# A fused attention and gated-MLP kernel: first loads spread over three queues, wk released by the landing of x, V's shifted copy by DMA, wd in four gated pieces

## Chip, cores, metric

One core of one Trainium2 chip. The metric is the device time of one execution in microseconds; lower is better.

## The reference, cut

```python
x = A_x                                     # (1, 2048, 512), bf16
g = sigmoid((x * gate_w).sum(-1, keepdims=True))
# A: 32 heads of 16; 4 segments of 512 rows
q, k, v = x @ wq, x @ wk, x @ wv
for s in range(4):
    p = softmax(q_s @ k_s.T * scale + causal_mask);  a_dot = p @ v_s
    a_mem = (phi(q_s) @ M) / (phi(q_s) @ z + 1e-6)      # memory of earlier segments
    o_s = gh * a_mem + (1 - gh) * a_dot
    M += phi(k_s).T @ v_s;  z += phi(k_s).sum(rows)
a = concat(o) @ wo
# B: gated MLP
b = (relu(x @ W_gate) * (x @ W_up)) @ W_down            # 512 -> 1792 -> 512
return g * a + (1 - g) * b
```

## The kernel before

The kernel describes its work as operations with estimated durations; a list scheduler, run when the program is built, gives each engine a fixed order, and the instructions are emitted in it. So a changed estimate, dependency or operation can reorder everything that comes after. TensorE runs in four modes: full 128-row matmuls, scores in four row strips, value products in 64x32 tiles, and column mode, for small products or for full ones cut into four column strips.

```python
MM = 0.216; SW = 0.1                       # a full matmul, a mode change, in us
...
for _ in range(28):                        # warm-up, on a tile that VectorE fills
    nc.tensor.matmul(g_dummy.t[:, 0:P], lhsT=zero[:, 0:P], rhs=zero[:, 0:P], ...)
...
for n, (c0, c1) in enumerate(((0, 1), (1, 2), (2, 4))):     # wq: three loads, GpSimd
    nc.gpsimd.dma_start(out=wq_sb[:, c0:c1, :], in_=A_wq[c0 * P:c1 * P, :]...)
...
o_wk0 = op("wk0", {"DVE": 0.08}, lambda e: nc.vector.memset(wk_sb[0:1, 0, 0:1], 0.0), ...)
lw["wk"].deps.append((o_wk0, None))        # wk is loaded after this write ...
o_wk0.deps.append((xc0[0][0], None))       # ... which follows the first copy of x transposed
...
def xload(s, key):                         # SyncE: x of a segment, transposed, then plain
    nc.sync.dma_start_transpose(out=xT[s].t[:], in_=x[s * L:(s + 1) * L, :])
    nc.sync.dma_start(out=xn[s].t[:], in_=...)
...
nc.sync.dma_start(out=wd_sb[:], in_=wview(B_W_down))        # wd: one load
...
nc.vector.scalar_tensor_tensor(xn[s].t[:, t, :], xn[s].t[:, t, :], 1.0, gwrep[:], ...)  # gate
...
nc.gpsimd.tensor_copy(VS[s].t[64 * r:64 * r + 64, t, ...], src[:, :, r, 0:DH])  # x 32
```

The softmax here doesn't subtract the row's maximum and nothing guards it: scores larger than these inputs give would overflow.

## Time and profile before

| what | before |
|---|---|
| median of 4 runs | 266.89 us (266.32 to 267.23) |
| span of the profiled run | 265.27 us |
| start, to the first matmul on wk | 9.60 us |
| list, from there to the last matmul's start | 252.26 us |
| end, from there to the end | 3.41 us |

The last three rows add up to the span: TensorE is full, so the start, the price of its list of instructions, and the end make the time.

### The profile page before, as it was taken

Reading aid. Unit: us, or ns where it says so; the run is one execution under the profiler, and the core shown is the slowest. Engines: PE = TensorE matmul, PEld = TensorE weight load, DVE = VectorE, ACT = ScalarE, POOL = GpSimd, SP = SyncE. Lnnn points to the kernel's source line nnn. Section 1 sums busy time; section 2 is a strip of 40 time slices with the busy share of each in tenths; the row PEclk is TensorE's granted clock in tenths of the full one; section 3 lists DMA queues with packets and bytes.
Section 4 is the critical chain, followed back from the end, with each engine's and each line's share of the span. In section 5 each row is a group of like instructions: output and inputs, shape, how many; then the busy total and the mean of one; then the engine's idle time right before and its main releaser. Section 6 shows DMA issues by size and latency. Waiting matters only on the chain.

```text
span 265.3 us, 7048 instructions
## 1 busy us (share of the span) xinstructions
PE 257.0 (97%) x2808; PEld 115.9 (44%) x2844; DVE 183.8 (69%) x407; ACT 193.9 (73%) x189; POOL 191.0 (72%) x470
## 2 busy tenths in 40 slices
PE   8999999999999999999999999999999999999995
PEld 6433444444454444444434434344443444344444
DVE  1497888888975285998888837688985735566611
ACT  3598999899885558999896668898788566777010
POOL 8678888888559788798648988887878866537000
PEclk9999999999999999999999999999999999999999
DMA  5997990017310100000551010000000010000011
GB/s 162 289 252 203 313 261 13 4 40 80 100 26 1 42 20 22 0 2 2 132 88 23 21 42 20 4 2 0 2 0 4 0 42 23 20 2 0 2 41 40
DMA packets 27057, 15.54 MB, mean 59 GB/s; under 512 B 13584, under 2 KB 26896, under 8 KB 27024
## 3 DMA queue, kind: packets, MB, share of 16 engines
q1 hardware_dynamic: 26304, 14.30, 22.0%
q0 software_dynamic: 176, 0.52, 0.6%
q8 instruction: 22, 0.36, 0.6%
q10 hardware_dynamic: 544, 0.26, 0.3%
q14 instruction: 11, 0.09, 0.1%
HBM read 9.84 MB, written 2.10 MB: 45 GB/s over the span
## 4 chain that ended last, share of the span: by engine, by line
PE 97%; issue 2%; DVE 0%; ACT 0%; DVEq 0%
PE G L248 74%; PE S L738 9%; PE G L849 7%; PE G L246 3%; PE S L406 2%; PE G L291 1%; PE G L611 1%; PE G L785 0%; PE G L385 0%; DVE os L700 0%; ACT xT L395 0%; DVE os L253 0%; DVE mcole L268 0%; DVEq L700 0%; DVE mcol L267 0%
## 5 line engine op out<-in xcount | busy, mean ns | idle before, releaser
L752 ACT ACTIVATE E<-S 128x2048 bf16<-128x2048 f32 x72 | 135.1, 1876 | 34.3 <-PE S L738 31.9
L760 POOL TENSOR_SCALAR_AFFINE_SELECT E<-E 64x256 bf16<-64x256 bf16 x256 | 115.7, 452 | 38.5 <-ACT E L752 24.6
L248 PE MATMUL G<-xT,wu_sb 128*128 128x512 bf16 x211 | 57.3, 380 | 0.4 <-issue 0.2
L248 PE MATMUL G<-xT,wg_sb 128*128 128x512 bf16 x206 | 56.2, 380 | 1.1 <-issue 0.8
L663 DVE TENSOR_TENSOR hT<-G,os 128x512 bf16<-128x512 f32 x56 | 38.2, 684 | 19.7 <-ACT os L659 10.7
L248 PE MATMUL G<-wd_sb,hT 128*128 128x512 bf16 (+1 forms) x212 | 48.9, 365 | 1.1 <-issue 1.0
L884 DVE STREAM_TRANSPOSE T<-G 128x512 f32<-128x512 f32 x44 | 30.3, 702 | 14.0 <-PE G L849 8.2
L659 ACT ACTIVATE os<-G 128x512 bf16<-128x512 f32 x56 | 32.7, 597 | 6.1 <-PE G L248 5.3
L248 PEld LDWEIGHTS <-wu_sb 128*128 128x128 bf16 x218 | 19.9, 98 | 24.8 <-issue 3.0
L248 PEld LDWEIGHTS <-wg_sb 128*128 128x128 bf16 x218 | 19.4, 98 | 24.6 <-issue 4.1
L248 PEld LDWEIGHTS <-hT 128*128 128x128 bf16 x222 | 20.3, 98 | 22.3 <-issue 2.6
L738 PE MATMUL S<-QT,K 32*128 32x192 bf16 (+7 forms) x512 | 28.6, 287 | 0.5
L738 PEld LDWEIGHTS <-K 32*128 32x128 bf16 x512 | 8.2, 92 | 30.4 <-issue 29.9
L700 DVE TENSOR_SCALAR os<-G,ngcol 128x512 bf16<-128x512 f32 (+1 forms) x10 | 7.0, 697 | 19.4 <-PE G L248 19.3
L849 PE MATMUL G<-E,Vp 64*32 64x128 bf16 (+7 forms) x512 | 19.0, 284 | 0.2 <-issue 0.2
L849 PE MATMUL G<-E,VS 64*32 64x128 bf16 (+7 forms) x512 | 18.4, 284 | 0.0
L248 PE MATMUL G<-wo_sb,oT 128*128 128x512 bf16 (+1 forms) x66 | 17.2, 367 | 0.3 <-issue 0.3
L597 POOL COPY VS<-Vp 64x256 bf16<-64x256 bf16 x32 | 13.3, 416 | 4.8 <-DVE Vp L515 3.3
L904 DVE TENSOR_TENSOR O<-T,sm 128x256 bf16<-128x256 f32 x32 | 15.8, 524 | 0.3
L248 PE MATMUL G<-xT,wk_sb 128*128 128x512 bf16 x60 | 15.8, 380 | 0.3 <-issue 0.2
L702 ACT ACTIVATE os<-G,ngcol 128x512 bf16<-128x512 f32 x7 | 4.8, 687 | 15.0 <-PE G L248 15.0
L479 POOL COPY R<-rcol 32x4 f32<-32x4 f32 x64 | 13.5, 210 | 3.0
(98 smaller groups left out, 302.0 us busy)
## 6 DMA issues: line engine op xcount, KB each, us to landing
out_dram<-os SPq DMA_DIRECT2D x15, 128.0 KB, 1.7
wd_sb<-in_B_W_down_dram SPq DMA_DIRECT2D x1, 1792.0 KB, 13.4
xn<-in_A_x_dram SPq DMA_DIRECT2D x3, 512.0 KB, 4.7
wg_sb<-in_B_W_gate_dram SPq DMA_DIRECT2D x2, 512.0 KB, 5.8
wu_sb<-in_B_W_up_dram SPq DMA_DIRECT2D x2, 512.0 KB, 6.9
wg_sb<-in_B_W_gate_dram SPq DMA_DIRECT2D x3, 256.0 KB, 6.9
wu_sb<-in_B_W_up_dram SPq DMA_DIRECT2D x3, 256.0 KB, 7.2
wk_sb<-in_A_wk_dram SPq DMA_DIRECT2D x1, 512.0 KB, 4.0
```

Source lines behind the costliest of these rows:

```text
L246: nc.tensor.matmul(out_ap[q], lhsT=lhsT[:, q], rhs=rhs, start=start, stop=stop, tile_position=(0, 32 * j))
L248: nc.tensor.matmul(out_ap, lhsT=lhsT, rhs=rhs, start=start, stop=stop)
L479: nc.gpsimd.tensor_copy(R[s][32 * j:32 * j + 32, k, :], rcol[32 * k:32 * k + 32, cols])
L597: nc.gpsimd.tensor_copy(VS[s].t[64 * r:64 * r + 64, t, 0:H // 2 * HP].rearrange("p (h v) -> p h v", v=HP)[:, :, 0:DH], src[:, :, r, 0:DH])
L659: nc.scalar.activation(rg.t[:], g.t[:], ACT.Relu)
L663: nc.vector.tensor_tensor(h.t[:], u.t[:], rg.t[:], ALU.mult)
L738: nc.tensor.matmul(sp.t[:, j, off:off + w], lhsT=K2[s, cc].t[rows, kb, :, :].rearrange("p r k -> p (r k)"), rhs=QT[s, cc].t[rows, L - w:L] ...
L752: nc.scalar.activation(eb_.t[:], sp.t[:], ACT.Exp, scale=SCALE)
L760: nc.gpsimd.affine_select(out=v, in_=v, compare_op=ALU.is_ge, fill=0.0, base=0, pattern=[[0, 4], [1, 64]], channel_multiplier=-1)
L849: nc.tensor.matmul(gs[r].t[32 * j:32 * j + 32, L - w:L], lhsT=v, rhs=src.t[rows, j, off:off + w], start=(kb == 0), stop=(kb == 7), tile_po ...
L884: nc.vector.transpose(T.t[:].rearrange("p b e -> p (b e)"), g.t[:])
L904: nc.vector.tensor_tensor(O.t[:, :, r, :], T.t[:, :, 0:DH], sm.t[:, r, :, None].to_broadcast([P, 16, DH]), ALU.mult)
```

## The change

Its intent: let TensorE's warm-up begin sooner, get x, wq and wk into place sooner, take 13 us of copies and 2 us of fills off GpSimd, keep the 1.8 MB of wd from blocking small transposes in the queue, and give the scheduler durations closer to the measured ones.

```diff
-MM = 0.216
-SW = 0.1
+MM = 0.2159
+SW = 0.094
+PX = 1.06                       # estimates of GpSimd times this
...
+    ones = nc.const_aps.tensor(1.0, [P, P], BF16)
-        for _ in range(28):      # on a tile filled by VectorE
+        for _ in range(31):      # on the constant
...
-    (x: two parts on SyncE, two on ScalarE; wq: three parts on GpSimd)
+    x0_part(0, 0, "SP", -300)
+    x0_part(0, 1, "ACT", -300)
+    wq_part(0, 1, "ACT", -299)
+    x0_part(1, 0, "SP", -299)
+    x0_part(1, 1, "POOL", -110)
+    wq_part(1, 2, "SP", -298)
+    wq_part(2, 4, "POOL", -80)
...
-    o_wk0 = ... nc.vector.memset(wk_sb[0:1, 0, 0:1], 0.0)      # after the first copy of xT
+    o_wk0 = ... nc.vector.tensor_copy(wk_sb[0:1, 0, 0:1], xn[0].t[0:1, 0, 0:1])   # after x landed
...
-        nc.sync.dma_start(out=wd_sb[:], in_=wview(B_W_down))
+    for c0, c1 in ((0, 4), (4, 8), (8, 12), (12, 14)):
+        gt = op(f"wd{c0}g", {"DVE": 0.08}, ... memset(wd_sb[0:1, c0, 0:1], 0.0) ...)
+        o = load(f"wd{c0}", ... wd_sb[:, c0:c1] ..., deps=[gt])
+    GATES = [(0, 1, 3), (0, 2, 1), (0, 2, 3), (0, 3, 1)]   # each gate waits for this exp
...
+            if ci == 0:          # two more warm-up matmuls ahead of the first on wq
+                for _ in range(2): nc.tensor.matmul(qS.t[:, 0, 0:P], lhsT=ones, rhs=ones, ...)
...
-        (VS: two buffers; 32 copies on GpSimd)
+            for r in range(2):   # one buffer, once a segment
+                nc.sync.dma_start(out=VS[s].t[a], in_=Vp[s].t[b])
```

More of the change, by code (lines that the diff above doesn't have):

```diff
@@ L26 @@
 VW = H * HP + 16
-VSW = H // 2 * HP + 16
-MM = 0.216
-SW = 0.1
+MM = 0.2159
+SW = 0.094
 MG = 1.0
+PX = 1.06
 class Buf:
@@ L63, in op @@
         o.flex, o.ran = flex, mode
+        engs = {e: d * (PX if e == "POOL" else 1.0) for e, d in engs.items()}
         o.name, o.engs, o.emit, o.key, o.cls, o.mode = name, engs, emit, key, cls, mode
@@ L219 @@
     Vpp = pool("Vp", 2, [P, 4, VW])
-    VSp = pool("VS", 2, [P, 4, VSW])
+    VSp = pool("VS", 1, [P, 4, VW])
     Ep = pool("E", 8, [P, 4, L])
@@ L225 @@
     osp = rgp = pool("os", 4, [P, D])
-    zero = osp.tiles[0]
     smp = pool("sm", 3, [P, 2, 16], F32)
@@ L249 @@
     ACTC = lambda n: 0.19 + 0.000833 * n
-    def c_zero(e):
-        nc.vector.memset(zero[:, 0:P], 1.0)
-    o_zero = op("zero", {"DVE": 0.15}, c_zero, cls=0, key=-100)
+    ones = nc.const_aps.tensor(1.0, [P, P], BF16)
+    o_zero = op("zero", {"DVE": 0.15}, lambda e: None, cls=0, key=-100)
     def c_ident(e):
@@ L262, in c_warm @@
     def c_warm(e):
-        nc.scalar.activation(scratch[:], zero[:, 0:1], ACT.Exp)
+        nc.scalar.activation(scratch[:], ones[:, 0:1], ACT.Exp)
     o_warm = op("warm", {"ACT": 1.5}, c_warm, deps=[o_zero], cls=0, key=-100)
@@ L274, in c_vones @@
     def c_vones(e):
-        for t in Vpp.tiles + VSp.tiles:
+        for t in Vpp.tiles:
             nc.gpsimd.memset(t[:].rearrange("p a b -> p (a b)"), 1.0)
-    o_vones = op("vones", {"POOL": 6.2}, c_vones, key=-60)
+    o_vones = op("vones", {"POOL": 4.2}, c_vones, key=-60)
     def c_bdm(e):
@@ L289, in c_dummy @@
     def c_dummy(e):
-        for _ in range(28):
-            nc.tensor.matmul(g_dummy.t[:, 0:P], lhsT=zero[:, 0:P], rhs=zero[:, 0:P], start=True, stop=True)
+        for _ in range(31):
+            nc.tensor.matmul(g_dummy.t[:, 0:P], lhsT=ones, rhs=ones, start=True, stop=True)
     g_dummy = Buf(G)
@@ L312, with first_load, x0_part, wq_part @@
     lx0, lw, lwq = {}, {}, {}
-    for i in range(2):
-        for eng, q, h in (("SP", nc.sync, 0), ("ACT", nc.scalar, 1)):
-            def f(e, i=i, q=q, h=h):
-                q.dma_start(out=xn[0].t[:, 2 * h:2 * h + 2, 256 * i:256 * i + 256],
-                            in_=x[256 * h:256 * h + 256, 256 * i:256 * i + 256].rearrange("(t p) d -> p t d", p=P))
-            lx0[i, h] = load(f"x0_{i}{h}", f, 131072, -300 + i, eng=eng, alloc=[xn[0]] if (i, h) == (0, 0) else [],
-                             uses=[] if (i, h) == (0, 0) else [xn[0]])
-    for n, (c0, c1) in enumerate(((0, 1), (1, 2), (2, 4))):
-        def f(e, c0=c0, c1=c1):
-            nc.gpsimd.dma_start(out=wq_sb[:, c0:c1, :], in_=A_wq[c0 * P:c1 * P, :].rearrange("(c p) n -> p c n", p=P))
-        o = op(f"wq{c0}", {"POOL": 1.0}, f, key=-110 + 15 * n, cls=0, land=131072 * (c1 - c0) / GBs)
+    QUEUE = {"SP": nc.sync, "ACT": nc.scalar, "POOL": nc.gpsimd}
+    def first_load(name, eng, key, nbytes, out_ap, in_ap, alloc=(), uses=()):
+        o = load(name, lambda e: QUEUE[eng].dma_start(out=out_ap(), in_=in_ap), nbytes, key, eng=eng, alloc=alloc, uses=uses)
+        if eng == "POOL":
+            o.engs["POOL"] = 0.9
+        return o
+    def x0_part(i, h, eng, key):
+        first = not lx0
+        lx0[i, h] = first_load(f"x0_{i}{h}", eng, key, 131072,
+                               lambda: xn[0].t[:, 2 * h:2 * h + 2, 256 * i:256 * i + 256],
+                               x[256 * h:256 * h + 256, 256 * i:256 * i + 256].rearrange("(t p) d -> p t d", p=P),
+                               alloc=[xn[0]] if first else [], uses=[] if first else [xn[0]])
+    def wq_part(c0, c1, eng, key):
+        o = first_load(f"wq{c0}", eng, key, 131072 * (c1 - c0), lambda: wq_sb[:, c0:c1, :],
+                       A_wq[c0 * P:c1 * P, :].rearrange("(c p) n -> p c n", p=P))
         for ci in range(c0, c1):
             lwq[ci] = [o]
+    x0_part(0, 0, "SP", -300)
[5 more added lines that the diff above has]
+    wq_part(2, 4, "POOL", -80)
     o_vones.deps.append((lwq[3][0], -1e9))
@@ L334 @@
     lw["wk"] = loadw("wk", wk_sb, A_wk, 0, D, 1)
-    o_wk0 = op("wk0", {"DVE": 0.08}, lambda e: nc.vector.memset(wk_sb[0:1, 0, 0:1], 0.0), key=-490, cls=0)
+    o_wk0 = op("wk0", {"DVE": 0.08}, lambda e: nc.vector.tensor_copy(wk_sb[0:1, 0, 0:1], xn[0].t[0:1, 0, 0:1]), key=-600, cls=0,
+               deps=[lx0[0, 0]], uses=[xn[0]])
     lw["wk"].deps.append((o_wk0, None))
@@ L369 @@
     lwo = loadw("wo", wo_sb, A_wo, 0, D, 3)
-    def f(e):
-        nc.sync.dma_start(out=wd_sb[:], in_=wview(B_W_down))
-    lwd = load("wd", f, P * NF * D * 2, 3)
+    lwd, wd_gate = {}, []
+    for c0, c1 in ((0, 4), (4, 8), (8, 12), (12, 14)):
+        gt = op(f"wd{c0}g", {"DVE": 0.08}, lambda e, c0=c0: nc.vector.memset(wd_sb[0:1, c0, 0:1], 0.0), key=-600, cls=0)
+        wd_gate.append(gt)
+        o = load(f"wd{c0}", lambda e, c0=c0, c1=c1: nc.sync.dma_start(out=wd_sb[:, c0:c1], in_=wview(B_W_down)[:, c0:c1]),
+                 P * (c1 - c0) * D * 2, 3, deps=[gt])
+        for fb in range(c0, c1):
+            lwd[fb] = o
     last_dma[0] = None
@@ L404, in f @@
         def f(e, ci=ci):
+            if ci == 0:
+                for _ in range(2):
+                    nc.tensor.matmul(qS.t[:, 0, 0:P], lhsT=ones, rhs=ones, start=True, stop=True)
             for c in range(NC):
@@ L407, in f @@
                                  start=(ci == 0), stop=(ci == NC - 1))
-        o_q0 = op(f"q0.{ci}", {"PE": 4 * MM * (1.5 if ci < 2 else 1)}, f,
+        o_q0 = op(f"q0.{ci}", {"PE": 4 * MM * (1.2 if ci < 2 else 1)}, f,
                   deps=xc0[ci] + lwq[ci] + [(o_q0, 0.0) if ci else None],
@@ L412 @@
             first_x(ci + 2, o_q0)
-    o_wk0.deps.append((xc0[0][0], None))
     xc0 = [o for c in range(NC) for o in xc0[c]]
@@ L419 @@
             for o in lx[s]:
-                o.deps.append((lwd, -1e9))
+                o.deps.append((lwd[NF - 1], -1e9))
         xr[s] = [lx[s][0]]
@@ L590, in proj_v, with f @@
                        uses=[g, Vp[s]])
-        if t == 0:
+        if t == 3:
             VS[s] = Buf(VSp)
-        o_vs[s, t] = []
-        for r in range(2):
-            def f(e, r=r):
-                src = Vp[s].t[64 - 64 * r:128 - 64 * r, t, 0:H * HP].rearrange("p (h r v) -> p h r v", r=2, v=HP)
-                nc.gpsimd.tensor_copy(
-                    VS[s].t[64 * r:64 * r + 64, t, 0:H // 2 * HP].rearrange("p (h v) -> p h v", v=HP)[:, :, 0:DH],
-                    src[:, :, r, 0:DH])
-            o_vs[s, t].append(op(f"vs{s}{t}{r}", {"POOL": 0.5}, f, deps=[o_v[s, t]] + (o_vs[s, t - 1] if t else []),
-                                 key=a.key + 4, cls=2, alloc=[VS[s]] if t == 0 and r == 0 else [],
-                                 uses=[Vp[s]] + ([] if t == 0 and r == 0 else [VS[s]])))
+            def f(e):
+                for r in range(2):
+                    a, b = slice(64 * r, 64 * r + 64), slice(64 - 64 * r, 128 - 64 * r)
+                    nc.sync.dma_start(out=VS[s].t[a], in_=Vp[s].t[b])
+            o_vs[s] = op(f"vs{s}", {"SP": 1.2}, f, deps=[o_v[s, t] for t in range(4)], key=a.key + 4, cls=0, land=2.5,
+                         alloc=[VS[s]], uses=[Vp[s]])
     W2 = 2 * (DH + 1)
@@ L641, in mz0 @@
         k = dkey(3)
-        a = op("mz0", {"PE": 0.5}, lambda e: mz_mm(0, g), deps=mz_deps(0), key=k, mode="C", alloc=[g], uses=[pK[0], Vp[0]])
+        a = op("mz0", {"PE": 0.56}, lambda e: mz_mm(0, g), deps=mz_deps(0), key=k, mode="C", alloc=[g], uses=[pK[0], Vp[0]])
         mz_after(0, a, g, k)
@@ L685, in dn @@
                 prev = op(f"d{s}{t}{hf}.{p0}", {"PE": (p1 - p0) * MM / halves}, f,
-                          deps=[lwd, (prev, 0.0) if prev else None] + gate + [o_h[s, fb] for fb in range(p0, p1)],
+                          deps=[lwd[p0], (prev, 0.0) if prev else None] + gate + [o_h[s, fb] for fb in range(p0, p1)],
                           key=dkey((p1 - p0) / halves), mode="D", flex="C", alloc=[g] if p0 == 0 else [],
@@ L741, in f @@
                                          tile_position=(32 * j, 0))
-            a = op(f"f{s}{c}.{n}", {"PE": MM}, f,
+            a = op(f"f{s}{c}.{n}", {"PE": 0.229}, f,
                    deps=[o_q[s, cc] for cc in chunks] + [o for cc in chunks for o in o_k2[s, cc]] +
@@ L753, in unit @@
             b = op(f"e{s}{c}.{n}", {"ACT": 1.88}, f, deps=[a], key=kf, cls=0, alloc=[eb_], uses=[sp])
+            if (s, c, n) in GATES:
+                wd_gate[GATES.index((s, c, n))].deps.append((b, None))
             offs = [p[2] for p in parts]
@@ L793, in dens @@
             gm = Buf(G)
-            rec_of[s, "mz"] = am = op(f"mz{s}", {"PE": 0.5}, lambda e: mz_mm(s, gm), deps=[(a, 0.0)], key=k0 - 20, mode="C",
+            rec_of[s, "mz"] = am = op(f"mz{s}", {"PE": 0.56}, lambda e: mz_mm(s, gm), deps=[(a, 0.0)], key=k0 - 20, mode="C",
                                       alloc=[gm], uses=[pK[s], Vp[s]])
@@ L842, in f @@
                     for j in range(4):
+                        h = 8 * c + 2 * j + r
                         if kb % 2 == r:
-                            h = 8 * c + 2 * j + r
                             v = Vp[s].t[rows, kb // 2, h * HP:h * HP + 32]
                         else:
-                            h = 4 * c + j
                             v = VS[s].t[rows, kb // 2, h * HP:h * HP + 32]
@@ L850, in f @@
                                          start=(kb == 0), stop=(kb == 7), tile_position=(64 * r, 32 * j))
-        a = op(f"pv{s}{c}", {"PE": 1.05}, f,
-               deps=[(m, MG) for m in masks] + [o_v[s, t] for t in range(4)] + [o for t in range(4) for o in o_vs[s, t]] +
+        a = op(f"pv{s}{c}", {"PE": 1.015}, f,
+               deps=[(m, MG) for m in masks] + [o_v[s, t] for t in range(4)] + [o_vs[s]] +
                ([(behind, 0.0)] if behind else []),
```

## The prediction

> **What bounds the kernel now.** I read the page of the profile first, then the list of waits for TensorE alone, then the stretches before, in and after its dense work, and last its instructions in order of time at the start. From the page:
>
> ```profile
> PE 257.0 (97%) x2808; PEld 115.9 (44%) x2844; DVE 183.8 (69%) x407; ACT 193.9 (73%) x189; POOL 191.0 (72%) x470
> ...
> PE   8999999999999999999999999999999999999995
> ...
> POOL 8678888888559788798648988887878866537000
> ...
> PE 97%; issue 2%; DVE 0%; ACT 0%; DVEq 0%
> ```
>
> TensorE is busy for 257.0 of 265.3 us, in every slice, and the chain that ended last runs through it for 97%. GpSimd, from which the change takes most, is busy for 72% and stands nowhere in that chain. A busy TensorE need not be at its peak, so I asked what it waited for (total us, times, longest):
>
> ```profile
> PE G L248 <- issue: 2.4, 15, 0.2
> PE G L291 <- DVE mcole L268: 1.1, 1, 1.1
> PE G L849 <- issue: 0.2, 1, 0.2
> ```
>
> After the first 1.1 us it waits for no transfer and for no other engine by any amount worth a row. The stretches (busy us of each engine in each):
>
> ```profile
> 0.00:1.12 1.12, 0.00 (x1) 0.01 (x1) 0.18 (x3) 0.00 (x0) 0.19 (x4) 1.00 0.00 0
> 1.12:9.60 8.48, 8.38 (x59) 5.97 (x61) 1.45 (x13) 3.02 (x6) 8.21 (x9) 1.00 0.73 234
> 9.60:262.10 252.50, 248.62 (x2750) 109.95 (x2783) 181.72 (x390) 190.93 (x183) 182.59 (x458) 1.00 0.22 53
> 262.10:265.30 3.20, 0.03 (x1) 0.00 (x0) 0.48 (x1) 0.00 (x0) 0.00 (x0) 1.00 0.07 20
> ```
>
> So the time is a start of 9.6 us, 252.5 us of TensorE instructions in a fixed order, and 3.2 us for the last eviction and store. A change shortens it only if it makes the start shorter, or the list of TensorE instructions cheaper. The start in order of time (start, duration, engine and line, count):
>
> ```profile
> 1.12 3.17 PE L291 MATMUL G<-os 128*128 128x128 bf16 x28 [1.12 <-DVE mcole L268]
> 4.08 1.06 PE L385 MATMUL G<-ident,xn 128*128 128x128 bf16 x8
> 5.18 1.54 PE L406 MATMUL S<-xT,wq_sb 128*128 128x512 bf16 x4
> 6.56 0.39 PE L385 MATMUL G<-ident,xn 128*128 128x128 bf16 x4
> 6.79 1.03 PE L406 MATMUL S<-xT,wq_sb 128*128 128x512 bf16 x4
> 7.65 0.39 PE L385 MATMUL G<-ident,xn 128*128 128x128 bf16 x4
> 7.87 1.89 PE L406 MATMUL S<-xT,wq_sb 128*128 128x512 bf16 x7
> 9.60 0.38 PE L248 MATMUL G<-xT,wk_sb 128*128 128x512 bf16 x1
> ```
>
> Here too TensorE is full, with one hole of 0.25 us ahead of 5.18. But it works slowly at first: the 28 warm-up matmuls start 107 ns apart, the transposes at 6.56 start 56 ns apart. The first four matmuls on wq take 5.18 to 6.56, the next four 6.79 to 7.65. The trace has the clock at full speed from 6.27 us. The landings of the loads are not in the way: x at 3.5 to 4.6 us, all well ahead of their transposes. Only wk is close: issued at 5.31, landed 4.03 us later at 9.34, and its first weights are loaded at 9.38.
>
> **What the skill says.** "TensorE: Matmul & The Clock Gate", Part 1, has TensorE at half clock until it has been busy through one window of about 3.4 us, which runs freely and does not begin with the kernel; 107 and 56 ns for 128 columns are its figures too, and the trace agrees. "TensorEngine Tiling (Array Packing)", Key Properties, says that changing the tiling mode drains the engine; the trace agrees: from the last full matmul to the first score matmul it is 312 ns, against 216 within a run, so 96 ns more. "DMA: Bandwidth & Descriptors", Rules for kernel authors, says that spreading loads over issuing engines does not add bandwidth and only saves issue time. This trace agrees in so far as an issue on SyncE takes about 0.5 us and loads queued behind each other land one by one.
>
> **The change, part by part.**
>
> *Warm-up.* The warm-up matmuls no longer read a tile that VectorE fills, but a constant written before the program's start. VectorE's fill ran from 0.89 to 1.06, so TensorE should start at about 0.92, 0.2 us sooner. There are 31 in place of 28: 3 x 107 ns = 0.32 us more. The transposes therefore come 0.12 us later; since that shift is in half-speed time, it is worth 0.06 us if the clock rises at the same moment. Two further matmuls of 128 columns (0.21 us) fall into the hole of 0.25 us. Busy 0.2 us sooner, TensorE may see the clock rise up to 0.2 us sooner, worth half: -0.1. Sum about -0.04 us.
>
> *wq and x over three queues.* x landed 0.3 us or more before its use and wq in time, so the reordering takes nothing from the path: 0.
>
> *wk held by the landing of x.* Its gate falls at about 3.6 us instead of 5.26, so it is issued some 1.6 us sooner and should land at 7.7 to 8.4 instead of 9.34. In the profiled run that uncovers only 0.04 us. But in a run where the clock rises sooner than 6.27, the queries would be done before 9.34, and wk would be the floor. Between no gain and about 0.4 us, by where the window falls: I put -0.15 on average.
>
> *V's shifted copy by DMA.* It takes 32 copies (13.3 us) and 2.3 us of fills off GpSimd. None lies on the path: 0. It adds two transfers per segment on SyncE, 64 x 4736 B each, 592 KB together. wk and wv (512 KB each) landed 1.45 us apart, so 592 KB is 1.7 us of transfer; 4.03 - 1.45 = 2.6 us is fixed; 4.3 us from issue to landing.
>
> *wd in four pieces.* It moves traffic out of the way of the transposes of K's features, which it delayed to 6.7 us from issue; TensorE waited for neither. 0.
>
> *The list of TensorE instructions.* The scheduler lays it out anew, and this I counted from the built programs: 2844 matmuls become 2759. Of these +5 are warm-up and -90 are 30 full matmuls that were issued as four column strips and no longer are (34 become 4). The useful work is the same. What a strip run costs shows in these two lines:
>
> ```profile
> 77.72 2.90 PE L246 MATMUL G<-wd_sb,hT 128*32 128x512 bf16 x48
> 80.56 0.40 PE L738 MATMUL S<-QT,K 32*128 32x320 bf16 x8
> ```
>
> 12 split matmuls take 80.56 - 77.72 = 2.84 us; 12 x 0.216 and a mode change of 0.096 are 2.69; 0.15 over. The other three such runs are over by 0.03, 0.03 and 0.01, so 0.22 for 34, and about -0.19 us for the 30 that go. Against this, the number of stretches in one mode rises from 171 to 174, and what follows what: with the trace's price of each kind of change (96 ns full to scores, 120 back, 93 full to value product, 118 scores to value product, 144 scores to strips, 106 strips to scores) the counts before give 18.48 us and after 18.71: +0.22 us.
>
> Sum: -0.04 - 0.15 - 0.19 + 0.22 = -0.16 us; 266.98 becomes 266.8.
>
> **Rivals.** *A new wait on the value copy.* There is now one buffer, so SyncE must wait for the last value product of a segment before it copies the next segment's, and the last transpose of K's features queues behind. In the new order the memory update that needs this transpose follows that product by 23 full matmuls and two score fills: 23 x 0.216 + 2 x 0.43 = 5.8 us. By the sizes above the transpose lands 4.3 + 0.5 = 4.8 us after. One us of slack: if a copy within SBUF ran at half the rate of a load, TensorE would wait about 0.7 us there, making 267.5. The second such place has 8 us.
>
> *The clock rises a whole window sooner.* If starting 0.2 us sooner tipped the window that ended near 2.9 us, the work from 2.9 to 6.3 would run at full speed, except that it waits for x to land at 3.5: up to 1.3 us, 265.6. TensorE was busy for only half of that window, and would be for 0.6 of it; unlikely.
>
> *A schedule that stops fitting.* The order is fixed from estimated durations, and TensorE takes it strictly. Gates for wd on VectorE wait for an exp on ScalarE and could hold evictions up. In the old kernel the same way of estimating left TensorE without waits, so I expect the new one to as well; if not, 268 to 270.
>
> *GpSimd as the real limit.* If its masks had set the pace, 15 us less on it would show as several us. Against it: TensorE has not one wait on it.
>
> **Range and chances.** Three runs of before spread over 0.9 us, which the window of the clock explains in size (3.4 us of phase at half speed is up to 1.7). I take 266.8 with 265.8 to 267.7. Two per cent is 5.3 us; the start as a whole is 9.6 and mostly untouched work, and nothing else is idle: faster 0.01. Slower by 5.3 us needs a broken schedule: 0.02.
>
> **What would show it.** The first warm-up matmul at about 0.9 us; the transposes near 4.2; the moment of the clock's rise, which I cannot place to better than a us; wk landed before 8.5; the first wk matmul at 9.3 to 9.7; strips of full matmuls down to 16; GpSimd busy for about 176 us and the time unmoved; no row for TensorE waiting on a transfer. A wait ahead of a memory update or a value product would show the first rival right; a TensorE total smaller by over 2 us without an earlier clock would prove my prices of the mode changes wrong.

## The result, and the profile after

The changed kernel's median is 267.98 us (267.61 to 268.29, 4 runs) against 266.89: ratio 1.0042, 95% interval 1.0021 to 1.0064, slower by 0.4%. Ratios are the mean time of one kernel's fast runs over that of the other's fast runs of the same rounds, so not quite the ratio of the medians quoted. The direction of the forecast was wrong, and the time lies above the forecast's range, though within 2% as forecast.

What TensorE waited for, in the changed kernel (total us, times, longest):

```profile
PE G L290 <- PEq L1030: 0.8, 1, 0.8
PE S L429 <- DMA wq_sb<-in_A_wq_dram: 0.3, 1, 0.3
PE G L248 <- DVE T L905: 0.2, 1, 0.2
```

The warm-up now starts at 0.83 us, as meant. But there are two new waits: one on wq in the start, and one on VectorE's transposes of value products, which lies in the middle. (The 2.4 us of "issue" in the old list are no waits: in that profile 36 of TensorE's 2844 matmul records are missing, in this one none. So TensorE's busy time and counts of matmuls can't be compared between the two.) The stretches, cut near the same events as before, to a tenth of a microsecond at the end:

```profile
0.83:9.54 8.71, 8.31 (x65) 6.08 (x66) 1.65 (x15) 2.91 (x6) 7.34 (x11) 1.00 0.80 248
9.54:262.50 252.96, 252.70 (x2695) 108.58 (x2693) 180.19 (x392) 192.60 (x185) 167.55 (x420) 1.00 0.26 62
262.50:265.90 3.40, 0.00 (x0) 0.00 (x0) 0.49 (x1) 0.00 (x0) 0.00 (x0) 1.00 0.07 19
```

The dense stretch grew from 252.50 to 252.96 us and the end from 3.20 to 3.40, while the start ends at 9.54 in place of 9.60. (Cut exactly at the last matmul's start, as in the first table, the list grew from 252.26 to 252.68 and the end from 3.41 to 3.69.) GpSimd went from 191.0 to 175.1 us busy, and nothing came of it. The start in order of time:

```profile
0.83 3.46 PE L290 MATMUL G<-const-bfloat16-1.0 128*128 128x128 bf16 x31 [0.83 <-PEq L1030]
...
5.12 1.02 PE L429 MATMUL S<-xT,wq_sb 128*128 128x512 bf16 x4
5.98 0.39 PE L405 MATMUL G<-ident,xn 128*128 128x128 bf16 x4
6.28 1.04 PE L429 MATMUL S<-xT,wq_sb 128*128 128x512 bf16 x4
7.16 0.39 PE L405 MATMUL G<-ident,xn 128*128 128x128 bf16 x4
7.81 1.90 PE L429 MATMUL S<-xT,wq_sb 128*128 128x512 bf16 x8 [0.26 <-DMA wq_sb<-in_A_wq_dram]
9.54 1.24 PE L248 MATMUL G<-xT,wk_sb 128*128 128x512 bf16 x5
```

In this run the clock was up at 4.44 us, 1.8 us sooner than in the profile before, and the first four matmuls on wq took 0.86 us instead of 1.38. That 0.5 us was lost again: the transposes at 7.16 end their starts at 7.32, and the matmuls on the last two blocks of wq begin at 7.81, when wq has landed.

The wait in the middle, in order of time, on VectorE and TensorE:

```profile
135.76 0.90 DVE L483 SCALAR_TENSOR_TENSOR xn<-xn,gwrep 128x512 bf16<-128x512 bf16 x1 [1.18 <-DMA xn<-in_A_x_dram]
...
136.59 0.71 DVE L905 STREAM_TRANSPOSE T<-G 128x512 f32<-128x512 f32 x1
...
136.99 0.38 PE L248 MATMUL G<-pq,M 128*128 128x512 bf16 x1
...
137.35 1.02 PE L248 MATMUL G<-xT,wg_sb 128*128 128x512 bf16 x4
...
138.62 0.38 PE L248 MATMUL G<-xT,wu_sb 128*128 128x512 bf16 x1 [0.25 <-DVE T L905]
```

VectorE stood still for 1.18 us because the plain load of x for the last segment had not landed (issued 129.69, landed 135.74). It could not be issued sooner, since SyncE takes its instructions in order: the transposing load of the same rows, which stands ahead of it, was issued only at 127.75. Behind it in VectorE's order stands the transpose of a value product that had just been finished. That transpose frees an accumulator, and TensorE needs accumulators: against its usual steps it lost 0.15 us after 136.99 and 0.41 after 138.00, together 0.56.

The tail, the last store of each kernel (issue, duration), with the span:

```profile
core 0 of [0], span 265.3 us
262.75 0.33 SPq L708 DMA_DIRECT2D out_dram<-os  x1
```
```profile
core 0 of [0], span 265.9 us
263.11 0.33 SPq L727 DMA_DIRECT2D out_dram<-os  x1
```

From issue to end it is 2.52 us before (first fence) and 2.79 after. The store lands 1.53 and 1.56 us after its issue; the rest is what follows it.

### The profile page after: what moved, and what is told of

Read it like the earlier page. It is cut to its first block, busy times and chain, and to the rows that moved or that the text cites. A ratio compares the mean times of both kernels' runs of the same rounds, so it can differ in the third digit from the quotient of the medians.

```text
span 265.9 us, 6922 instructions
## 1 busy us (share of the span) xinstructions
PE 261.0 (98%) x2759; PEld 114.7 (43%) x2759; DVE 182.3 (69%) x408; ACT 195.5 (74%) x191; POOL 175.1 (66%) x435
## 4 chain that ended last, share of the span: by engine, by line
PE 92%; DMA 4%; DVE 1%; POOL 1%; issue 0%; SPq 0%; POOLq 0%; DVEq 0%
PE G L248 75%; PE S L758 9%; PE G L870 6%; DMA xn<-in_A_x_dram 2%; DMA wq_sb<-in_A_wq_dram 2%; PE S L429 1%; PE G L630 1%; DVE xn L483 1%; DVE T L905 0%; PE G L807 0%; PE G L246 0%; POOL xn L315 0%; DVE os L719 0%; POOL ident L257 0%; POOL ident L256 0%
## 5 line engine op out<-in xcount | busy, mean ns | idle before, releaser
L248 PE MATMUL G<-xT,wu_sb 128*128 128x512 bf16 x224 | 59.8, 380 | 0.2 <-DVE T L905 0.2
L248 PE MATMUL G<-xT,wg_sb 128*128 128x512 bf16 x224 | 59.3, 380 | 0.0
L248 PE MATMUL G<-wd_sb,hT 128*128 128x512 bf16 (+1 forms) x234 | 53.9, 367 | 0.0
L248 PEld LDWEIGHTS <-hT 128*128 128x128 bf16 x234 | 21.4, 98 | 23.7 <-issue 2.8
L248 PEld LDWEIGHTS <-wg_sb 128*128 128x128 bf16 x224 | 20.2, 98 | 25.5 <-issue 3.9
L248 PE MATMUL G<-wo_sb,oT 128*128 128x512 bf16 (+1 forms) x68 | 18.0, 368 | 0.0
L248 PE MATMUL G<-xT,wk_sb 128*128 128x512 bf16 x64 | 16.5, 379 | 0.0
L947 POOL TENSOR_TENSOR O<-O,O 128x512 bf16<-128x512 bf16 x11 | 13.1, 1186 | 4.8 <-DVE O L925 4.1
```

Source lines behind the costliest of these rows:

```text
L248: nc.tensor.matmul(out_ap, lhsT=lhsT, rhs=rhs, start=start, stop=stop)
L947: (nc.vector if e == "DVE" else nc.gpsimd).tensor_tensor(Oa.t[:], Oa.t[:], Ob.t[:], ALU.add)
```

## The experiments

The accounts to test, beside noise. **S**, start: wq lands late, because of where it is issued (S1) or because the early wk takes its bandwidth (S2). **D**: the halt at 137 us comes from VectorE held by x. **L**: the new TensorE order is itself dearer. **T**: the end is longer by its construction. Where I say "TensorE's order is the changed kernel's", I compared the two built programs and they agree instruction by instruction.

### after_again: the changed kernel unaltered

> The changed kernel unaltered, for its spread and a second profile. Its first profile has four terms against the kernel before: first wk matmul 9.54 us against 9.60, the list of TensorE instructions from there to the last matmul 252.7 against 252.3, of which 0.56 is a halt at 137 us, and 3.69 against 3.41 from the last matmul to the end. If the list (theory L) and the halt (theory D: VectorE held by a late x) are systematic, the list is 252.6 to 252.8 again and the halt 0.4 to 0.7 at the same place; if the end (theory T) is systematic, it is over 3.6 again. Theory S, the start: the first wk matmul cannot come before about 9.5 however early the clock rises, because wq comes late. Ratio 1.002 to 1.006.

267.91 us (266.58 to 268.62) against 267.09; ratio 1.0023, interval 0.9999 to 1.0047. The second profile, of a run of 268.62, has start 10.21, list 253.04, end 3.67. The halt is there again, 0.97 us in its two parts, the end too. New is a wait in the start:

```profile
PE G L248 <- DMA wk_sb<-in_A_wk_dram: 1.0, 1, 1.0
```

wk, issued at 3.64, landed only at 10.16. So D and T are systematic, and the new start varies.

### wq_pool: the place of the wq issues undone

```diff
-    wq_part(0, 1, "ACT", -299)
+    wq_part(0, 1, "POOL", -110)
-    x0_part(1, 1, "POOL", -110)
-    wq_part(1, 2, "SP", -298)
+    x0_part(1, 1, "ACT", -299)
+    wq_part(1, 2, "POOL", -95)
```

> The three parts of wq all issued by GpSimd and the fourth part of x by ScalarE, as before the change; TensorE's order is the changed kernel's to the instruction. If the place of the wq issues makes wq late (S1), its last two blocks are in use from at most 7.4 us when the clock rises early, and the first wk matmul comes at 9.2 or sooner, 0.1 to 0.4 us of time gained at most. If it is the early wk that takes their bandwidth (S2), wq's last blocks come at 7.6 or later still and the first wk matmul stays at 9.5 or later. The list stays at 252.7.

267.22 us (266.81 to 268.01), ratio to before 1.0008 (0.9991 to 1.0025). First wk matmul at 9.17 with the clock up at 5.37; wq's last blocks in use from 7.45, without a wait; list 252.68, end 3.70. These look like S1's numbers, but the landings do not bear S1 out: wq's last two blocks landed at 7.38 here, and at 7.76 and 7.11 in the changed kernel's two profiles. TensorE came to them only at 7.45 here, so it did not wait. In time it is 0.7 below the changed kernel of the same rounds, but the two intervals overlap, and the profiles bear out 0.3 of it.

### wk_late: wk's gate undone

```diff
-    ... tensor_copy(wk_sb[0:1, 0, 0:1], xn[0].t[0:1, 0, 0:1]), key=-600 ... deps=[lx0[0, 0]]
+    ... memset(wk_sb[0:1, 0, 0:1], 0.0), key=-490, cls=0)
+    o_wk0.deps.append((xc0[0][0], None))
```

> wk held until the first copy of transposed x, as before the change; the rest is the changed kernel, TensorE's order the same. Under S2 (wk takes wq's bandwidth) the last two blocks of wq land by 7.0 and TensorE has no wait on wq there, but wk itself then lands at 9.2 to 9.4 and is the floor: first wk matmul 9.4 to 9.6, time within 0.2 us of the changed kernel. Under S1 the wait on wq's last blocks stays at 0.2 us or more.

267.69 us (267.32 to 268.54), ratio 1.0028 (1.0009 to 1.0047). wk landed at 9.43 and the first wk matmul came at 9.48 after a wait of 0.2; the wait on wq was gone, and the last packet of GpSimd's loads ended at 6.03 us, against 7.34 and 6.77 in the changed kernel's two profiles. The landings of wq's last two blocks (us) in all 14 profiles tell the two accounts apart:

| | wq over three queues | wq on GpSimd |
|---|---|---|
| wk early | 7.76, 7.11, 7.49, 7.28, 7.26, 6.73 | 7.38, 7.41, 7.33, 6.74 |
| wk late | 6.42 | 6.43, 6.38, 6.30 |

(First row: after, after_again, xn_first, lanes, vs_pool, wd_early; then wq_pool, combined, combined_again, before_start. Second row: wk_late; then before, before_again, before_warm.)

So S2 holds: an early wk delays wq by about 0.9 us, and a late one becomes the floor. S1, the place of the issues, is not shown: it moves the landing by less than the profiles scatter. Taking one gate back changes one wait for another.

### xn_first: the plain load of x ahead of the transposing one

```diff
-            nc.sync.dma_start_transpose(out=xT[s].t[:], ...)
+            (nc.sync.dma_start(out=xn[s].t[:], ...) if s > 1 else None); nc.sync.dma_start_transpose(out=xT[s].t[:], ...)
```

> For the last two segments the plain load of x is issued ahead of the transposing load instead of after it; nothing else moves, and the four engines' orders are those of the changed kernel. Theory D: VectorE no longer waits on x (1.2 us in the changed kernel), the halt of TensorE at 137 to 138.6 us goes, the list takes 252.1 to 252.2 and the time falls by 0.5 to 0.6 us, ratio to before about 1.002. Rival: the halt comes from the value transposes themselves, and 252.7 stays.

266.72 us (266.60 to 267.51), ratio 0.9994 (0.9976 to 1.0012); list 252.13 in place of 252.68, and TensorE's only listed wait is the 0.8 before its first instruction. x is issued at 121.21 and landed at 125.24, nine us ahead of its use. The same TensorE instructions as above:

```profile
136.73 0.38 PE L248 MATMUL G<-pq,M 128*128 128x512 bf16 x1
136.94 1.03 PE L248 MATMUL G<-xT,wg_sb 128*128 128x512 bf16 x4
137.81 0.38 PE L248 MATMUL G<-xT,wu_sb 128*128 128x512 bf16 x1
```

The steps between these three are 0.21 and 0.87 us, against 0.36 and 1.27: 0.55 us regained. D is shown. The time fell by more than that (1.2 in medians of the same rounds); the remainder is within the spread.

### lanes: five more transfers, so that the last store gets another semaphore

```diff
-    lwo = loadw("wo", wo_sb, A_wo, 0, D, 3)
+    lwo = load("wo", ... two halves ...)
-    ... dma_start(out=wd_sb[:, c0:c1], ...)
+    ... each piece as two halves ...
```

> Each of the four wd transfers and the one of wo is issued as two halves; nothing else moves. With five more transfers the last store falls on the last of the eight semaphores that SyncE goes through at the end, in place of the third. Theory T: the end is longer because SyncE, after the last landing, still goes through five waits of 62 ns that are long satisfied; then last matmul to end falls from 3.68 to 3.35-3.42 us, the list stays 252.7 with its halt at 137 us, and the time falls by 0.3. Rival: the store itself lands later in the new kernel; then 3.6 or more stays.

267.06 us (266.12 to 267.91), ratio 0.9995 (0.9968 to 1.0022). The end is 3.33 us, against 3.69 and 3.67; the halt is there, 0.97 us as in after_again (list 253.10), and in this profile the clock rose only at 6.59 (start 9.77). The last store:

```profile
core 0 of [0], span 266.2 us
...
263.76 0.33 SPq L727 DMA_DIRECT2D out_dram<-os  x1
```

2.44 us from issue to end. SyncE's own records tell why. In the built program, the transfers of SyncE and ScalarE use eight semaphores in turn. At the end SyncE waits for them one after the other, a wait every 62 ns even where it is long satisfied. In the kernel before, five such waits ran while the last store was under way and one came after; in the changed one, with more transfers, the last store's semaphore is the first waited for, and five come after. T is shown, and it has nothing to do with the store. Two runs made for other ends agree: wd_early, with three transfers fewer, has the last store on the last semaphore again and an end of 3.32; vs_pool, with eight fewer and so the same semaphore as the changed kernel, has 3.69.

### vs_pool: V's copy back on GpSimd

```diff
-                    nc.sync.dma_start(out=VS[s].t[a], in_=Vp[s].t[b])
+                    nc.gpsimd.tensor_copy(...)          # eight a segment, in one block
```

> The changed kernel with V's shifted copy back on GpSimd (eight copies a segment at the place where SyncE issued its transfer, and a fill of the buffer at the start); TensorE's, VectorE's and ScalarE's orders are the changed kernel's. If GpSimd is off the path, as predicted, the list stays within 0.1 of 252.7 plus or minus what the traffic on SyncE did: theory D2 says that the transfers of V's copy do not cause the halt at 137 us, so it stays at 0.5. Rival: GpSimd's 3.5 us in one block delay masks and hence value products; then TensorE shows waits ahead of them and the list is over 253. GpSimd busy rises by 13 to 16 us.

268.04 us (267.62 to 268.52), ratio 1.0038 (1.0013 to 1.0063); GpSimd busy 190.0 us. My D2 failed: the halt at 137 is gone, since x landed 0.5 us sooner after the first wk matmul and VectorE waited 0.39. Why it landed sooner is open, since V's transfers of this stage are issued only after x has landed (135.93 in the changed kernel). But the rival's halt took its place, though behind an addition on GpSimd rather than a mask:

```profile
PE G L248 <- DVE oT L954: 0.5, 1, 0.5
```

At 148 us TensorE stood about 0.7 us for the transposed output that waits for that addition, and at 43.9 another 0.23 for an exp that frees a score buffer; list 253.09. In this TensorE order GpSimd's relief may therefore be worth something. But the experiment puts the copies in one block, which is harsher than the kernel before was; there, spread out, they kept TensorE waiting nowhere in its profiles.

### wd_early: wd as one transfer, ungated

```diff
-    lwo = loadw("wo", ...)
+    lwo = load("wo", ... dma_start(wo_sb ...), dma_start(out=wd_sb[:], in_=wview(B_W_down)))
-    (the four pieces and their gates)
```

> wd as one transfer of 1792 KB right behind wo and without gates, as before the change, in the changed kernel's TensorE order. It is issued at about 27 us and holds the queue until about 40, so the two transposes of K's features that the memory product at 40.2 us needs land at 40.3 to 40.8 in place of 36.0 and 39.2. If the gates matter for the new order, TensorE waits 0.2 to 0.8 us ahead of that product and the time rises by as much; if they do not, no wait and 267.9 as for the changed kernel.

269.09 us (267.72 to 271.67), ratio 1.0085 (1.0042 to 1.0128).

```profile
PE G L630 <- DMA pK<-pk: 1.7, 2, 1.5
```

The two transposes landed at 41.68 and 42.11, later than I had it, and the memory product needed them at 39.8. Against xn_first TensorE lost 2.0 us at that product, and the halt near 137 grew to 1.05. In time the difference to the 267.9 of the changed kernel is 1.2 us, of other rounds, and two of the six runs (270.56 and 271.67) had a granted clock of only 0.99; the other four have a mean of 268.5. So the gates are worth 2 us of waits in the profile and 0.6 to 1.2 us in time to the new order. They buy back what that order itself asks for: the old one put this product at 42.4 and had the transposes at 40.7 with wd in front of them.

### before_again: the kernel before, a second profile

> The kernel before, unaltered, for a second profile. Its first profile had 9.60 us to the first wk matmul with the clock up at 6.27, a list of 252.26 us of which 0.34 is one halt inside a value product at 45.7 us, and 3.41 at the end. If theory L holds (the new order of TensorE is itself dearer, by 0.2), the list is 251.9 to 252.3, against 252.13 in the changed kernel's order without its halt, and 251.9 if the halt at 45.7 does not recur. If the old list is 252.1 or more without a halt, L falls. The end is 3.38 to 3.44.

266.71 us, one run. Clock up at 4.87, start 9.41 (held 0.2 by wk, landed 9.36), list 252.19, end 3.41. The halt inside the value product recurs, 0.35 us at 45.4. Without it the old order takes 251.84 and 251.92 in the two profiles (251.84 in this one), against 252.13 for the new one without a halt: L is 0.2 to 0.3 us.

### before_warm: the new warm-up alone on the kernel before

```diff
-        for _ in range(28): ... lhsT=zero[:, 0:P] ...
+        for _ in range(31): ... lhsT=ones ...       # and two ahead of the first query matmul
```

> The kernel before with the new warm-up alone: matmuls on a constant, 31 of them, and two ahead of the first query matmul. If the warm-up is worth what was predicted (0.04 us, plus up to 0.4 where wk allows it), the first wk matmul is at 9.4 to 9.7 with the clock up between 4.4 and 6.3, held by wk landing at 9.3 to 9.5; ratio to before 0.998 to 1.001. The list stays as before.

267.13 us (266.42 to 267.65), ratio 1.0015 (1.0000 to 1.0031). The clock was up at 3.68, but the start is 9.28, sooner than I had put it: TensorE waited 0.3 for wq and 0.3 for wk. A clock that rises 2.6 us sooner than in the first profile gained 0.3 us of start. The list is 252.66 there, with a halt of 0.55 us at 45.3, so the length of that halt varies. A second wait is new: VectorE stood 1.5 us at 137 us for a transpose of K's features, and TensorE lost 0.24 at 138.7. So the old order, too, seems to be held by a transfer through VectorE in some runs; its two unaltered profiles do not show it.

### before_start: the new warm-up and wk's new gate on the kernel before

```diff
+    (as before_warm)
-    ... memset(wk_sb[0:1, 0, 0:1], 0.0), key=-490 ...; o_wk0.deps.append((xc0[0][0], None))
+    ... tensor_copy(wk_sb[0:1, 0, 0:1], xn[0].t[0:1, 0, 0:1]), key=-600 ... deps=[lx0[0, 0]]
```

> The same with wk held by the landing of x instead of the first copy; wq stays on GpSimd and everything after the start is the kernel before. By theory S the start alone, with wq where it was, is a gain: wk lands at 8.1 to 8.9, the first wk matmul is at 9.1 to 9.3 with a clock up by 5.5 us, list 251.9 to 252.3, end 3.4, time 0.2 to 0.4 below before, ratio 0.997 to 1.000. If an early wk slows wq (S2), the first wk matmul stays at 9.5.

267.05 us (266.56 to 267.30), ratio 1.0007 (0.9992 to 1.0022): no gain in time. wk landed at 8.48, no wait in the start, but the clock rose at 6.40 in the profiled run and the first wk matmul came at 9.68. That profile cannot decide S, which was about an early clock; list 252.34, with VectorE's wait for a transpose of K's features (1.3 us) and TensorE's loss of 0.24 as in before_warm; end 3.42.

### combined and combined_again: the three repairs together

wq_pool, xn_first and split transfers in one kernel; wo goes in three parts here and not in two, since wq_pool has one transfer fewer on these semaphores.

> The changed kernel with the start's issues as before (wq on GpSimd), the plain x ahead of the transposing one, and the transfers split so that the last store has the last semaphore. If the three terms add: first wk matmul at 9.1 to 9.3 with an early clock, list 252.1 to 252.2, end 3.35 to 3.42, sum 264.6 to 264.9 us of span, about 266.3 us, ratio to before 0.996 to 0.999. If they do not add, because one wait hides another, 266.8 or more.

266.58 us (266.14 to 267.08), ratio 0.9981 (0.9959 to 1.0003). First wk matmul 9.19 (clock up at 4.50), list 252.13, end 3.35: 264.67 us of span.

> The three repairs together once more, on another chip if it falls so, because the first interval (0.9959 to 1.0003) just holds 1. List 252.1 to 252.2 without a wait, end 3.35, first wk matmul 9.1 to 9.5, ratio 0.996 to 0.999.

266.62 us (266.26 to 267.01) against 266.70, ratio 0.9996 (0.9982 to 1.0010). Start 9.12 (this trace has no record of the clock, and TensorE waited 0.3 for the first block of wq), list 252.13, end 3.33, and the dense stretch has no halt:

```profile
9.12:261.52 252.40, 252.39 (x2695) 108.59 (x2693) 179.16 (x392) 192.55 (x185) 167.28 (x421) 1.00 0.25 62
```

In the profiles the list and the end add as meant: 264.6 us of span against 265.0 and 265.3 for the kernel before. That the start of 9.1 to 9.2 is wq's doing is not shown (see below). In time it is 1.3 to 1.4 us below the medians of the changed kernel, which are of other rounds, but no version is shown to beat the kernel before: both intervals hold 1.

## Why the prediction was wrong

The two unaltered pairs of profiles, in us:

| | before (2 profiles) | changed (2 profiles) | difference of means |
|---|---|---|---|
| start | 9.60, 9.41 | 9.54, 10.21 | +0.37 |
| list | 252.26, 252.19 | 252.68, 253.04 | +0.63 |
| end | 3.41, 3.41 | 3.69, 3.67 | +0.27 |
| span | 265.27, 265.01 | 265.90, 266.92 | +1.27 |

**The step that failed most: "In the old kernel the same way of estimating left TensorE without waits, so I expect the new one to as well."** The new order places the work on the last segment's x on VectorE at 126 us after the first wk matmul, where the old one had it at 134. The load could not be there: it was issued at 120.2 behind a transposing load and landed at 126.2 to 126.6. VectorE waited 1.2 and 1.7 us, TensorE 0.56 and 0.97. I had looked only for waits of TensorE on transfers, and for gates on VectorE; a load that holds VectorE, and through it the accumulators, I did not follow. xn_first shows it. Nor was the old order free of waits: it has a halt of its own, 0.34 and 0.35 at 45.5, which I read past in a row of 0.2 ("issue"), and in before_warm and before_start another, of 0.24. What causes the halt at 45.5 is open.

**"3.2 us for the last eviction and store"** was taken as untouched. The number of transfers on SyncE and ScalarE changed from 55 to 67, with it the semaphore of the last store, and with that the end: +0.27. lanes shows it. It was to be had from the built program before the run.

**The list, "-0.19" and "+0.22".** The sum of +0.03 measured +0.2 to +0.3, halts taken off both. The counts were right (2844 to 2759 matmuls, 34 cut ones to 4, 171 stretches to 174); the prices were not. Measured in the profiles with all records (before_again, xn_first, combined_again), from matmul start to matmul start and with the last matmul's own time taken off (216 ns for 512 columns, fewer in proportion), a change of mode costs 95 ns on average and 90 to 106 by kind. My 120, 118 and 144 are whole steps, which still hold the last score matmul's own 27 to 54 ns, set beside 96 and 93, which do not. The 170 changes of the old order cost 16.12 us and the 173 of the new one 16.47: +0.35 in place of +0.22. The cut matmuls, small products included, give about -0.10 in place of -0.19 (-0.04 to -0.14 by the old profile taken). These two make the +0.2 to +0.3.

**The start, "-0.15" for wk, "-0.04" for the warm-up, "0" for wq.** TensorE did start at 0.83. But wq did not stay in time: the early wk delayed its last blocks by about 0.9 us, so that in the first profile they were usable at 7.81, where the slower clock before had used them at 7.87, and the earlier clock gained nothing. wk landed at 9.07 and 10.16 in place of "7.7 to 8.4", and at 8.10 to 8.92 in the eight other profiles with its new gate, presumably since it shares the transfer engines with wq: my figure took over the 4.03 us of a wk loaded late. Over the six profiles with the changed kernel's unaltered start (these two, xn_first, lanes, vs_pool, wd_early) the first wk matmul came at 8.97 to 10.21, 9.51 in the mean; 9.50 in the two of the kernel before. So the start gained nothing on average, and the +0.37 of the table is in part the luck of two profiles. With wq on GpSimd and wk early it was 9.12, 9.17 and 9.19 in the changed order, but 9.68 in before_start, where the clock rose late; so a gain from wq's place is not shown.

**What held.** GpSimd's relief (175.1 us, "about 176") moved nothing. The first rival did not come: TensorE never waited for V's copy. But "4.8 us" after the value product, with "one us of slack", was luck in part. Measured, the last transpose landed at 79.62, 5.8 us after the value product's last matmul started, and was needed at 79.92, so 0.3 was left. The second such place had 0.5, not "8 us". wd's pieces, "0", are right for the comparison of the two kernels, but the new order depends on them.

Together: the table's list and end, with the start at its mean over all profiles, make 0.9 of the median's 1.1 us. What stays open: how much of the rest is the start, whose single runs scatter by a microsecond with the clock and the landings.

## What to carry to other kernels

When one engine is full and the order is fixed ahead, freeing another engine that it does not wait for gains nothing (16 us less on GpSimd gained none here), and every estimate that moves an instruction forward must be checked against the landing of what it reads, on every engine that holds a shared buffer, not on the full engine alone. A load that is brought forward takes bandwidth from the loads that are needed first. Look at the end of the program too: the number of transfers alone can move it by a quarter of a microsecond.

## What the Trainium skill lacked or had wrong

- No page that I read has that the end of a program grows with the place of the last transfer's semaphore among eight: the waits come 62 ns apart, and the end was 3.32 to 3.42 or 3.67 to 3.70 us.
- "TensorE: Matmul & The Clock Gate" puts the clock's rise after one busy window of about 3.4 us. Here the clock was up 2.85 us after the first matmul (before_warm: 0.83 to 3.68) at the soonest, and 5.8 us after it (lanes) at the latest. 2.85 us is less than the page's window, so that window was not busy all through; its length fits, as the full-speed stretches recorded here last 259.41 or 262.83 us and differ by 3.42.
- "TensorEngine Tiling (Array Packing)" says that a change of mode drains the engine, without a price; here it is 95 ns on average (96 from full matmuls to score matmuls, 90 to 106 by kind).
- "DMA: Bandwidth & Descriptors" has no figure for a plain load between transposing ones. 512 KB of x took 3.9 to 4.0 us from issue to landing ahead of the transposing load of x, 4.3 to 4.7 behind it in the old order, and 6.0 to 6.9 in the new one (5.1 in vs_pool), where a transpose of K's features was issued 0.7 us behind it. Which of the neighbours slows it was not tested.
